# Another order for the first block's units, and numerators between gate and value, in a fused attention and feed-forward kernel

## The chip, the cores and the metric

The kernel runs on one core of a Trainium2 chip. The metric is the device time of one execution in microseconds. The kernel before takes 328.98 us, the median of three runs (328.57 to 329.07).

The core has five engines that run at the same time, each with its own queue in program order: TensorE (PE in the profile, its weight loads PEld), VectorE (DVE), ScalarE (ACT), GpSimd (POOL) and SyncE (SP), which here only issues transfers. They wait for each other by semaphores. TensorE writes to PSUM, a memory of eight banks of 512 fp32 values in each of 128 partitions.

## The reference

```
q, k, v: [8, 8, 576, 64]        # batch, heads, sequence, head size
phi(x) = [relu(x) cos(w), relu(x) sin(w)]    # w = pi/2 * pos/576, 128 features
kv  = phi(k)^T v                # per batch and head, 128 x 64
z   = sum over positions of phi(k)
num = phi(q) kv;  den = phi(q) z + 1e-6
x   = num / den, heads side by side          # [4608, 512]
g = x w_gate;  val = x w_val                 # 512 -> 1536
out = (gelu(g) * val) w_out                  # 1536 -> 512, float32
```

## The kernel before

The 4608 tokens of x are cut into nine blocks: block 0 has the 576 tokens of batch 0, blocks 1 to 7 have 512 tokens each, and block 8 the last 448 (`starts`, `ends`, L44). x is kept transposed, `xT`, with 512 features in four groups of 128 partitions.

**Feed-forward.** A unit is one of the 12 tiles of 128 hidden features (`jt`) for a stretch of tokens of a block. `gate` (L213) runs four matmuls into one PSUM bank and lets ScalarE take the gelu of it into a `gel` buffer, of which three rotate. `value` (L224) runs four matmuls into another bank, and VectorE multiplies that bank by the `gel` buffer into `hT` (L233). `gv_unit` is a gate and then a value; a list `mid` of functions can be called between the two, and nothing passes one in the kernel before. `o_tile` multiplies 128 tokens of `hT` by `w_out` (L258), ScalarE copies the bank, and SP stores it.

**Attention.** For each batch, `scale` computes phi for k and q (L134 on VectorE, L136 on ScalarE), and `cast_v` the bf16 values with a column of ones. `kv_half` computes kv and z for four heads in a bank (L153). A numerator step is `numer` (L192): `numer_mm` (L167, its matmuls L169) runs four matmuls of 65 columns into each of two neighbouring banks; then `norm` on VectorE takes the denominators (den, L181), their reciprocals (rec, L183) and the quotient (xb, L184). xb must be transposed to become a part of xT. In block 0 and for batch 1 this is done by PE (`x_by_pe`, L342, with a copy out of the bank in L345); for later batches SP issues a DMA transpose (`turn_x`, L204). The features of q are transposed in the same two ways (`q_by_pe` with `q_evac`, L323 and L331; `turn_q`, L144).

**Order.** All of it is written out by hand: the program order of each engine is that of the code. Block 0 begins while the weights are still being loaded by POOL in pieces (`load_w`: tiles 0 and 1, then 2 and 3, 4 to 7, 8 to 11). So its first units are small pieces of 128 tokens, each run as soon as its part of xT is there, from L408. There, `X(t, ...)` is the transpose of xb of token tile t, `Y(t, bank)` is the numerator step of tile t in that bank and the next, A stands for tokens 0 to 255 and `Bw` for 256 to 575. From tile 4 on a loop (L467) runs the remaining units in the two pieces A and Bw. Then comes the attention of batch 1, interleaved with the output tiles of block 0.

In blocks 1 to 6, `run_block(n)` runs the 12 units, gate banks 0 and 1, value banks 2 and 3 in turn. After each unit it calls what `after[n][jt]` holds: scales, transposes and loads of a later batch, `attn_step(b, 0)` (the two `kv_half`, banks 6 and 7), then in five further units `attn_step(b, i)` (a numerator step in banks 6 and 7 and its `turn_x`), and output tiles of the block before. In block 1 everything is one unit earlier, and the load of the next q comes in unit 5.

Buffers exist once for q, k and v in fp32 (`qf`, `kf`, `vf`), so a load is issued when the last reader is done. `dummies` are matmuls on a zeroed buffer `junk` that fill PE's waits at the start.

Of the kernel before, what the change touches and what calls it, by code (L numbers as in the profile page):

```python
# [9 lines left out]
FP32 = mybir.dt.float32  # L10
BF16 = mybir.dt.bfloat16
# [5 lines left out]
def kernel(  # L17
# [18 lines left out]
    JT = J // 128  # L36
# [9 lines left out]
    NB = len(starts)  # L46

    ctx.enter_context(tc.manual_schedule())
    sb = ctx.enter_context(tc.tile_pool(name="sb", bufs=1))
    rot = ctx.enter_context(tc.tile_pool(name="rot", bufs=2))  # L50
# [16 lines left out]
    kv = [sb.tile([128, H, D + 2], BF16, name=f"kv{i}") for i in range(2)]  # L67

    hT = [sb.tile([128, JT, 64 + 576], BF16, name=f"hT{i}") for i in range(2)]
    ident = sb.tile([128, 128], BF16, name="ident")  # L70
    junk = sb.tile([128, 512], BF16, name="junk")
    tiny = sb.tile([1, 8], FP32, name="tiny")


# [54 lines left out]
    def scale(f, j, which, eng, h0=0, h1=H):  # L129
        dst, src = f  # L130
        col = (cos_c if which == 0 else sin_c)[:, j:j + 1]
        s, d = src[:, h0:h1, j, :], dst[:, j, h0:h1, which * D:(which + 1) * D]
        if eng == "v":
            nc.vector.tensor_scalar(d, s, col, 0.0, op0=ALU.mult, op1=ALU.max)  # L134
        else:
            nc.scalar.activation(d, s, AF.Relu, scale=col)  # L136
# [55 lines left out]
    def numer(b, t, bank, rows=128):  # L192

        numer_mm(b, t, bank, 0, rows)
        numer_mm(b, t, bank, 1, rows)
        xb = new_xb()
        norm(xb, bank, 0, 2, rows)
        return xb
# [12 lines left out]
    gels = {}  # L211

    def gate(n, jt, c0, w, gb):  # L213

        p0 = starts[n] + c0
        for ct in range(CT):
            nc.tensor.matmul(  # L217
                ps[:, gb, 0:w], lhsT=wg_sb[:, ct, jt * 128:(jt + 1) * 128],
                rhs=xT[:, ct, p0:p0 + w], start=(ct == 0), stop=(ct == CT - 1),
            )  # L220
        gels[n, jt, c0] = gel = rot.tile([128, 512], FP32, name="gel", bufs=3)
        nc.scalar.activation(gel[:, 0:w], ps[:, gb, 0:w], AF.Gelu)  # L222

    def value(n, jt, c0, w, vb):  # L224

        p0 = starts[n] + c0
        for ct in range(CT):
            nc.tensor.matmul(  # L228
                ps[:, vb, 0:w], lhsT=wv_sb[:, ct, jt * 128:(jt + 1) * 128],
                rhs=xT[:, ct, p0:p0 + w], start=(ct == 0), stop=(ct == CT - 1),  # L230
            )
        gel = gels.pop((n, jt, c0))
        nc.vector.tensor_mul(hT[n % 2][:, jt, 64 + c0:64 + c0 + w], gel[:, 0:w], ps[:, vb, 0:w])  # L233

    def gv_unit(n, jt, c0, w, gb, vb, mid=()):
        gate(n, jt, c0, w, gb)
        for f in mid:
            f()
        value(n, jt, c0, w, vb)

    def carry(n):

        w = ends[n] - starts[n]
        nc.gpsimd.tensor_copy(hT[(n + 1) % 2][:, :, 0:64], hT[n % 2][:, :, w:w + 64])  # L244
# [74 lines left out]
    def q_by_pe(b, j, bank, eng, h0=0, h1=H):  # L319

        qb = ps[:, bank, :].bitcast(BF16).rearrange("p (h t) -> p h t", h=H)
        for h in range(h0, h1):
            nc.tensor.transpose(out=qb[:, h, :], in_=qp[:, j, h, :], identity=ident)  # L323
        if eng is not None:
            q_evac(b, j, bank, eng, h0, h1)

    def q_evac(b, j, bank, eng, h0=0, h1=H):
        qb = ps[:, bank, :].bitcast(BF16).rearrange("p (h t) -> p h t", h=H)
        cp = nc.vector.tensor_copy if eng == "v" else nc.scalar.copy
        if j < NJ:  # L330
            cp(qT[b % 2][:, j, h0:h1], qb[:, h0:h1])  # L331
        else:
            cp(qT[b % 2][:, j, h0:h1, 0:64], qb[:, h0:h1, 0:128:2])

    def x_by_pe(b, t, xb, bank, eng, c0=0, c1=CT, every=1):
        p0 = b * S + t * 128
        cp = nc.vector.tensor_copy if eng == "v" else nc.scalar.copy
        xb2 = xb.rearrange("p g h d -> p (g h d)")
        rows = 128 if t < NJ or every == 2 else 64
        view = ps[:, bank, 0:256].bitcast(BF16).rearrange("p (c t) -> p c t", c=CT)  # L340
        for ct in range(c0, c1):
            nc.tensor.transpose(  # L342
                out=view[:, ct, 0:rows], in_=xb2[0:rows, ct * 128:(ct + 1) * 128], identity=ident[0:rows, 0:rows],
            )
        cp(xT[:, c0:c1, p0:p0 + rows // every], view[:, c0:c1, 0:rows:every])  # L345

    def sq(j, which, eng, *h):
        scale(Q, j, which, eng, *h)
# [48 lines left out]
    A, Bw = (0, 256), (256, 320)  # L397
    xs = {1: x1}

    def X(t, bank, eng):  # L400
        return lambda: x_by_pe(0, t, xs[t], bank, eng)

    def Y(t, bank):
        def f():
            xs[t] = numer(0, t, bank, 128 if t < NJ else 64)
        return f

    gate(0, 0, 0, 128, 5)  # L408
    gate(0, 1, 0, 128, 4)
    X(1, 2, "v")()  # L410
    q_evac(0, 2, 3, "v")
    sq(3, 0, "v"), sq(3, 1, "s")
    value(0, 0, 0, 128, 6)
    value(0, 1, 0, 128, 7)
    gate(0, 0, 128, 128, 5)
    gate(0, 1, 128, 128, 4)
    sq(4, 1, "s"), sq(4, 0, "v")
    value(0, 0, 128, 128, 6)
    value(0, 1, 128, 128, 7)
    Y(2, 2)()  # L420
    q_by_pe(0, 3, 0, "s")
    q_by_pe(0, 4, 1, "v")
    gv_unit(0, 2, *A, 4, 6)
    X(2, 0, "s")()
    Y(3, 2)()
    gv_unit(0, 3, *A, 5, 7)
    gv_unit(0, 0, 256, 128, 4, 6)
    X(3, 1, "v")()
    Y(4, 2)()
    gv_unit(0, 1, 256, 128, 5, 7)  # L430
    gv_unit(0, 0, 384, 128, 4, 6)
    gv_unit(0, 1, 384, 128, 5, 7)
    X(4, 0, "v")()
    gate(0, 4, *A, 3)
    gv_unit(0, 2, *Bw, 4, 6)
    gv_unit(0, 3, *Bw, 5, 7)
    value(0, 4, *A, 1)
    gv_unit(0, 0, 512, 64, 0, 2)
    gv_unit(0, 1, 512, 64, 4, 6)


    load_q(1, nc.gpsimd)
# [7 lines left out]
    def L(f, *a):  # L450
        return lambda: f(*a)
# [14 lines left out]
    }  # L466
    for jt in range(4, 12):  # L467
        for i, (c0, w) in enumerate((A, Bw)):
            if (jt, i) != (4, 0):
                gv_unit(0, jt, c0, w, i, 3 - i)  # L470
            for f in between.get((jt, i), ()):
                f()
# [49 lines left out]


    after = {n: {jt: [] for jt in range(JT)} for n in range(NB)}
    for n in range(1, 7):
        b = n + 1
        a = after[n]

        def put(u, *fs):
            a[u].extend(fs)  # L530

        s = 0 if n > 1 else -1
        if n > 1:
            put(0, L(sq, 0, 0, "v"), L(sq, 1, 0, "v"), L(sq, 1, 1, "v"), L(sq, 0, 1, "s"))
            put(1, L(sq, 2, 0, "v"), L(sq, 2, 1, "s"), L(turn_q, b, 0, 3))
            put(1, L(sq, 3, 0, "v"), L(sq, 4, 0, "v"), L(sq, 4, 1, "v"), L(sq, 3, 1, "s"), L(turn_q, b, 3, 5))
        else:
            put(0, L(sq, 1, 1, "s"), L(sq, 2, 1, "v"), L(turn_q, b, 0, 3))
            put(0, L(sq, 3, 1, "v"), L(sq, 4, 1, "s"), L(turn_q, b, 3, 5))
        put(2 + s, L(sk, 0, 0, "v"), L(sk, 1, 0, "v"), L(sk, 0, 1, "s"), L(sk, 1, 1, "s"))  # L540
        put(3 + s, L(sk, 2, 0, "v"), L(sk, 3, 0, "v"), L(sk, 4, 0, "v"))
        put(3 + s, L(sk, 2, 1, "s"), L(sk, 3, 1, "s"), L(sk, 4, 1, "s"), L(cast_v, b, 0, 4))
        put(4 + s, L(cast_v, b, 4, 8, "s"))
        put(5 + s, L(attn_step, b, 0))
        if b + 1 < B:

            for f, u in zip((load_q, load_k, load_v), (3, 4, 5) if n > 1 else (5, 10, 11)):
                put(u, L(f, b + 1))
        for i in range(5):
            put(6 + s + i, L(attn_step, b, i + 1))  # L550

    for n in range(2, NB):
        for i, m in enumerate(o_tiles_of(n - 1)):
# [2 lines left out]
    def run_block(n):  # L556
        w = ends[n] - starts[n]
        for jt in range(JT):
            gv_unit(n, jt, 0, w, jt % 2, 2 + jt % 2)
            for f in after[n][jt]:  # L560
                f()
        if n + 1 < NB:
            carry(n)

    for n in range(1, NB):
        run_block(n)
# [34 lines left out]
```

## Time and profile before

| | us |
|---|---|
| median of three runs | 328.98 |
| the profiled execution's own time | 328.85 |
| its span | 326.7 |
| PE busy | 316.8 |
| DVE busy | 172.1 |
| ACT busy | 150.4 |
| POOL busy | 21.5 |

The span is the time from the first to the last recorded instruction; what lies around it is in the execution's own time only. Matmuls overlap: each is shown for 0.38 us at 512 columns, while four follow each other in 0.86 us, so a PE that is shown as busy may still be late, and start times are what to read. A row of the timeline has the start in us from the span's start, the length in us, the engine, the line, the operation, what it writes and reads, the count that was merged, and in brackets the idle time before it with the work that ended it. A row of the waits has the engine and line that waited, what for, the sum in us, how often, and the longest.

### The profile page before, as it was taken

The page shows a single profiled execution, that of the slowest core. Times are in us where ns is not written, and L with a number is a line of the kernel's source. Part 1 is how long each engine was busy: PE and PEld are TensorE (multiplying, and loading weights), DVE is VectorE, ACT ScalarE, POOL GpSimd, SP SyncE. Part 2 cuts the span into 40 slices and gives each one's busy share as a digit, 9 for nine tenths or more (in the row PEclk, how much of TensorE's full clock was granted, in tenths as well). Part 3 has the DMA queues.
Part 4 walks back from the last instruction along what each step waited for, and adds up shares of the span by engine and source line. Part 5 has one row for each costly group of instructions (what it writes and reads, how often), then busy time and mean ns, then how long its engine had stood idle before and what let it go on. Part 6 is the DMA issues. An engine that isn't in the chain of part 4 may idle for free.

```text
span 326.7 us, 5828 instructions
## 1 busy us (share of the span) xinstructions
PE 316.8 (97%) x2188; PEld 167.4 (51%) x2222; DVE 172.1 (53%) x383; ACT 150.4 (46%) x269; POOL 21.5 (7%) x41
## 2 busy tenths in 40 slices
PE   7999999999999999999999999999999999999994
PEld 2587866554445544544454445444554444444543
DVE  5795676868753667365835484548455222322210
ACT  6564664772474256424652375237622332223321
POOL 2650010000100010001000010001000100100000
PEclk9999999999999999999999999999999999999999
DMA  7999999996799938992699459984623211000024
GB/s 228 284 205 274 222 302 299 315 220 122 216 269 293 283 69 162 305 272 67 131 300 294 81 104 232 341 132 84 144 52 78 44 36 34 32 32 32 34 65 96
DMA packets 87739, 55.42 MB, mean 170 GB/s; under 512 B 52512, under 2 KB 82976, under 8 KB 87712
## 3 DMA queue, kind: packets, MB, share of 16 engines
q1 hardware_dynamic: 81200, 48.71, 59.7%
q0 software_dynamic: 6080, 5.90, 10.1%
q10 hardware_dynamic: 432, 0.46, 0.4%
q8 instruction: 17, 0.28, 0.3%
q14 instruction: 10, 0.08, 0.1%
HBM read 37.75 MB, written 9.44 MB: 144 GB/s over the span
## 4 chain that ended last, share of the span: by engine, by line
PE 91%; DVE 3%; DMA 2%; issue 1%; SPq 1%; POOL 0%; ACT 0%; DVEq 0%; POOLq 0%
PE ps L217 28%; PE ps L258 28%; PE ps L228 27%; PE ps L169 3%; PE ps L153 3%; DMA vf<-in_v_dram 2%; SPq L79 1%; DVE hT L233 1%; PE ps L276 1%; PE ps L342 1%; PE ps L323 1%; DVE xb L184 1%; DVE qp L134 0%; DVE rec L183 0%; DVE vx L140 0%
## 5 line engine op out<-in xcount | busy, mean ns | idle before, releaser
L233 DVE TENSOR_TENSOR hT<-gel,ps 128x512 bf16<-128x512 f32 (+5 forms) x126 | 76.4, 610 | 128.6 <-PE ps L228 121.8
L228 PE MATMUL ps<-xT,wv_sb 128*128 128x512 bf16 (+5 forms) x492 | 111.8, 348 | 1.1 <-DVE hT L233 0.8
L217 PE MATMUL ps<-xT,wg_sb 128*128 128x512 bf16 (+5 forms) x490 | 111.8, 348 | 1.0
L222 ACT ACTIVATE gel<-ps 128x512 f32<-128x512 f32 (+5 forms) x126 | 67.5, 536 | 77.6 <-PE ps L217 75.3
L258 PE MATMUL ps<-wo_sb,hT 128*128 128x512 bf16 x413 | 95.5, 379 | 0.6
L228 PEld LDWEIGHTS <-wv_sb 128*128 128x128 bf16 x504 | 47.9, 98 | 47.1 <-issue 1.0
L217 PEld LDWEIGHTS <-wg_sb 128*128 128x128 bf16 x504 | 45.7, 98 | 40.6 <-DVE xT L345 0.4
L258 PEld LDWEIGHTS <-hT 128*128 128x128 bf16 x420 | 40.1, 98 | 45.4
L287 ACT COPY o_sb<-ps 128x512 f32<-128x512 f32 x35 | 20.5, 585 | 75.4 <-PE ps L258 74.4
L184 DVE TENSOR_TENSOR xb<-ps,rec 128x512 bf16<-128x512 f32 (+2 forms) x41 | 27.8, 678 | 1.7 <-DVE rec L183 0.2
L136 ACT ACTIVATE kp<-kf,sin_c 128x512 bf16<-128x512 f32 (+1 forms) x41 | 25.4, 681 | 0.2 <-DMA kf<-in_k_dram 0.2
L134 DVE TENSOR_SCALAR qp<-qf,cos_c 128x512 bf16<-128x512 f32 x40 | 20.2, 546 | 0.0
L169 PEld LDWEIGHTS <-qT 128*128 128x128 bf16 (+1 forms) x320 | 15.0, 98 | 9.1 <-issue 2.3
L136 ACT ACTIVATE qp<-qf,sin_c 128x512 bf16<-128x512 f32 x28 | 19.3, 713 | 0.2 <-DMA qf<-in_q_dram 0.2
L134 DVE TENSOR_SCALAR kp<-kf,cos_c 128x512 bf16<-128x512 f32 (+1 forms) x45 | 18.7, 463 | 0.8 <-DMA kf<-in_k_dram 0.7
L169 PE MATMUL ps<-kv,qT 128*128 128x65 bf16 (+1 forms) x320 | 16.5, 193 | 0.5 <-DVE xb L184 0.3
L208 POOL COPY xT<-xr 128x256 bf16<-128x256 bf16 x6 | 2.4, 400 | 200.4 <-DMA xr<-xb 200.4
L153 PEld LDWEIGHTS <-kp 128*128 128x128 bf16 x320 | 10.9, 97 | 2.9 <-issue 1.0
L126 PE MATMUL ps<-junk 128*128 128x512 bf16 x33 | 10.5, 470 | 1.8 <-DVE par_i L103 1.7
L153 PE MATMUL ps<-vx,kp 128*128 128x65 bf16 x320 | 11.1, 193 | 0.4 <-DVE vx L140 0.4
L140 ACT CAST vx<-vf 128x1280 bf16<-128x1280 f32 (+1 forms) x9 | 9.7, 1076 | 1.6 <-DMA vf<-in_v_dram 1.6
L244 POOL COPY hT<-hT 128x768 bf16<-128x768 bf16 x8 | 7.6, 946 | 37.9 <-DVE hT L233 37.9
(55 smaller groups left out, 88.3 us busy)
## 6 DMA issues: line engine op xcount, KB each, us to landing
out_dram<-o_sb SPq DMA_DIRECT2D x38, 128.0 KB, 2.4
kf<-in_k_dram SPq DMA_DIRECT2D x7, 640.0 KB, 7.9
out_dram<-o_sb SPq DMA_DIRECT2D x16, 256.0 KB, 3.2
qf<-in_q_dram SPq DMA_DIRECT2D x6, 640.0 KB, 6.1
vf<-in_v_dram SPq DMA_DIRECT2D x6, 640.0 KB, 9.5
kf<-in_k_dram SPq DMA_DIRECT2D x7, 512.0 KB, 6.4
qf<-in_q_dram SPq DMA_DIRECT2D x6, 512.0 KB, 5.0
vf<-in_v_dram SPq DMA_DIRECT2D x6, 512.0 KB, 8.5
```

The source lines that it names most:

```text
L126: nc.tensor.matmul(ps[:, bank, :], lhsT=junk[:, 0:128], rhs=junk, start=True, stop=True)
L134: nc.vector.tensor_scalar(d, s, col, 0.0, op0=ALU.mult, op1=ALU.max)
L136: nc.scalar.activation(d, s, AF.Relu, scale=col)
L153: nc.tensor.matmul(ps[:, bank, (h % 4) * (D + 1):(h % 4 + 1) * (D + 1)], lhsT=kp[:, j, h, :], rhs=vx[b % 2][:, j, h, 0:D + 1], start=(j == ...
L169: nc.tensor.matmul(ps[0:rows, bank + g, (h % 4) * (D + 1):(h % 4 + 1) * (D + 1)], lhsT=qT[b % 2][:, t, h, 0:rows], rhs=kv[b % 2][:, h, 0:D ...
L184: nc.vector.tensor_tensor(xb[0:rows, g0:g1], nd[:, :, :, 0:D], rec[0:rows, 0:n, :, None].to_broadcast([rows, n, 4, D]), op=ALU.mult,)
L217: nc.tensor.matmul(ps[:, gb, 0:w], lhsT=wg_sb[:, ct, jt * 128:(jt + 1) * 128], rhs=xT[:, ct, p0:p0 + w], start=(ct == 0), stop=(ct == CT - 1),
L222: nc.scalar.activation(gel[:, 0:w], ps[:, gb, 0:w], AF.Gelu)
L228: nc.tensor.matmul(ps[:, vb, 0:w], lhsT=wv_sb[:, ct, jt * 128:(jt + 1) * 128], rhs=xT[:, ct, p0:p0 + w], start=(ct == 0), stop=(ct == CT - 1),
L233: nc.vector.tensor_mul(hT[n % 2][:, jt, 64 + c0:64 + c0 + w], gel[:, 0:w], ps[:, vb, 0:w])
L258: nc.tensor.matmul(ps[:, bank, :], lhsT=hT[n % 2][:, jt, c0:c0 + 128], rhs=wo_sb[:, jt, :], start=(jt == 0), stop=(jt == JT - 1),)
L287: nc.scalar.copy(o_sb, ps[:, bank, :])
```

## The change

Four things change.

1. In block 0 the hand-written order of the first units is another one. The numerators of tile 2 are put ahead of the second gates, those of tile 3 between gate and value of unit 3. The numerators use banks 0 and 1 in place of 2 and 3, transposes and values other banks too, and gates keep to 4 and 5 nearly throughout. Some copies out of PSUM go from VectorE to ScalarE and the other way. The A piece of tile 5 is run there too, so that the loop skips it.
2. In blocks 1 to 6 the five numerator steps with their `turn_x` are called between gate and value of their unit, and no longer after it.
3. `gel` has four buffers in place of three.
4. `junk` is no buffer of its own but a part of `hT[1]`.

On SP one step moves: in block 1 the first `turn_x` comes ahead of the two transfers of `load_q(3)`.

```diff
+    junk = hT[1][:, 0, 0:512]
     ident = sb.tile([128, 128], BF16, name="ident")
-    junk = sb.tile([128, 512], BF16, name="junk")
...
-        gels[n, jt, c0] = gel = rot.tile([128, 512], FP32, name="gel", bufs=3)
+        gels[n, jt, c0] = gel = rot.tile([128, 512], FP32, name="gel", bufs=4)
...
     gate(0, 0, 0, 128, 5)
     gate(0, 1, 0, 128, 4)
-    X(1, 2, "v")()
+    X(1, 2, "s")()
     q_evac(0, 2, 3, "v")
     sq(3, 0, "v"), sq(3, 1, "s")
     value(0, 0, 0, 128, 6)
     value(0, 1, 0, 128, 7)
+    Y(2, 0)()
     gate(0, 0, 128, 128, 5)
     gate(0, 1, 128, 128, 4)
+    value(0, 0, 128, 128, 2)
+    value(0, 1, 128, 128, 3)
+    q_by_pe(0, 3, 6, "s")
+    gate(0, 2, *A, 5)
+    X(2, 0, "v")()
     sq(4, 1, "s"), sq(4, 0, "v")
-    value(0, 0, 128, 128, 6)
-    value(0, 1, 128, 128, 7)
-    Y(2, 2)()
-    q_by_pe(0, 3, 0, "s")
-    q_by_pe(0, 4, 1, "v")
-    gv_unit(0, 2, *A, 4, 6)
-    X(2, 0, "s")()
-    Y(3, 2)()
-    gv_unit(0, 3, *A, 5, 7)
-    gv_unit(0, 0, 256, 128, 4, 6)
-    X(3, 1, "v")()
-    Y(4, 2)()
-    gv_unit(0, 1, 256, 128, 5, 7)
-    gv_unit(0, 0, 384, 128, 4, 6)
-    gv_unit(0, 1, 384, 128, 5, 7)
+    value(0, 2, *A, 7)
+    gate(0, 3, *A, 4)
+    Y(3, 0)()
+    value(0, 3, *A, 2)
+    q_by_pe(0, 4, 3, "s")
+    gv_unit(0, 0, 256, 128, 5, 6)
+    X(3, 0, "s")()
+    Y(4, 0)()
+    gv_unit(0, 1, 256, 128, 4, 7)
+    gv_unit(0, 0, 384, 128, 5, 2)
+    gv_unit(0, 1, 384, 128, 4, 3)
+    gate(0, 4, *A, 5)
     X(4, 0, "v")()
-    gate(0, 4, *A, 3)
-    gv_unit(0, 2, *Bw, 4, 6)
-    gv_unit(0, 3, *Bw, 5, 7)
-    value(0, 4, *A, 1)
-    gv_unit(0, 0, 512, 64, 0, 2)
-    gv_unit(0, 1, 512, 64, 4, 6)
+    gate(0, 5, *A, 4)
+    gv_unit(0, 2, *Bw, 1, 6)
+    gv_unit(0, 3, *Bw, 0, 7)
+    value(0, 4, *A, 3)
+    value(0, 5, *A, 2)
+    gv_unit(0, 0, 512, 64, 4, 6)
+    gv_unit(0, 1, 512, 64, 5, 7)
...
-            if (jt, i) != (4, 0):
+            if (jt, i) not in ((4, 0), (5, 0)):
                 gv_unit(0, jt, c0, w, i, 3 - i)
...
+    mid = {n: {jt: [] for jt in range(JT)} for n in range(NB)}
...
         for i in range(5):
-            put(6 + s + i, L(attn_step, b, i + 1))
+            mid[n][6 + s + i].append(L(attn_step, b, i + 1))
...
-            gv_unit(n, jt, 0, w, jt % 2, 2 + jt % 2)
+            gv_unit(n, jt, 0, w, jt % 2, 2 + jt % 2, mid[n][jt])
```

## The prediction

> **What bounds the kernel now.** I read the page's busy times first, then the chain that ended last, then busy time by stage, the waits of TensorE (PE) and the timeline around them.
>
> ```profile
> span 326.7 us, 5828 instructions
> PE 316.8 (97%) x2188; PEld 167.4 (51%) x2222; DVE 172.1 (53%) x383; ACT 150.4 (46%) x269; POOL 21.5 (7%) x41
> ...
> PE 91%; DVE 3%; DMA 2%; issue 1%; SPq 1%; POOL 0%; ACT 0%; DVEq 0%; POOLq 0%
> ```
>
> PE is the bound almost everywhere. Only time in which PE does not issue can be won. By stage (columns: stretch, its length, busy us and count of each engine, clock, DMA share, GB/s):
>
> ```profile
> 0.00:16.60 16.60, 14.07 (x117) 7.20 (x119) 11.17 (x40) 10.39 (x20) 7.67 (x21) 1.00 1.00 255
> 16.60:33.25 16.65, 15.70 (x204) 12.95 (x202) 11.58 (x34) 8.52 (x22) 4.05 (x6) 1.00 1.23 239
> ...
> 60.20:83.90 23.70, 23.27 (x175) 11.86 (x177) 17.98 (x40) 14.00 (x24) 0.00 (x0) 1.00 0.81 189
> 83.90:117.50 33.60, 33.34 (x220) 16.57 (x224) 18.60 (x40) 16.18 (x27) 1.17 (x2) 1.00 1.00 263
> 117.50:273.00 155.50, 154.46 (x976) 75.70 (x993) 82.80 (x169) 70.64 (x118) 6.62 (x10) 1.00 0.65 151
> ```
>
> A busy PE can still be late, because matmuls overlap. So I went by start times: a 512-column matmul should follow the last by 0.216 us (four in 0.86), 320 columns by 0.136, 256 by 0.109, 128 by 0.056, 65 by 0.032. A longer step is a stall. Single steps of twice the length, with a record missing, are not counted. The first stage (to 16.60) is not touched by the order of the change. After 273 nothing is.
>
> **Blocks 1 to 6.** The waits view between 60 and 270 us has, for PE and its weight loads, only the numerators (L169):
>
> ```profile
> PEld L169 <- issue: 1.9, 7, 0.6
> ```
>
> The costliest one, in block 1:
>
> ```profile
> 72.39 0.69 DVE L233 TENSOR_TENSOR hT<-gel,ps 128x512 bf16<-128x512 f32 x1 [2.23 <-PE ps L169]
> 72.87 1.03 PE L228 MATMUL ps<-xT,wv_sb 128*128 128x512 bf16 x4
> 73.00 0.16 DVE L181 TENSOR_SCALAR den<-ps 128x8 f32<-128x8 f32 x1
> ...
> 73.43 0.69 DVE L184 TENSOR_TENSOR xb<-ps,rec 128x512 bf16<-128x512 f32 x1
> ...
> 74.17 0.42 PE L169 MATMUL ps<-kv,qT 128*128 128x65 bf16 x8 [0.28 <-DVE xb L184]
> ```
>
> The four value matmuls from 72.87 end their issue at 72.87 + 0.864 = 73.73. The next numerator starts at 74.17, after xb (end 74.12) has emptied banks 6 and 7: 0.44 lost. The same sum at the other six places gives 0.07 (77.9), 0.07 (109.0), 0.26 (142.8), 0.07 (176.4), 0.07 (210.0), 0.07 (243.7): **1.05 us**. The 0.44 and 0.26 are larger because DVE itself started late there (product at 72.39 where 72.0 was possible; 0.23 idle between rec and xb at 142.05).
>
> **Block 0, 16.6 to 33.25.**
>
> ```profile
> 19.28 0.61 PE L228 MATMUL ps<-xT,wv_sb 128*128 128x128 bf16 x8 [0.56 <-DVE hT L233]
> ...
> 23.61 0.40 PE L342 MATMUL ps<-ident,xb 128*128 128x128 bf16 x4
> 23.93 0.44 PE L169 MATMUL ps<-kv,qT 128*64 128x65 bf16 x8
> ...
> 25.84 0.38 PE L228 MATMUL ps<-xT,wv_sb 128*128 128x128 bf16 x4 [0.24 <-DVE hT L233]
> ```
>
> Late steps: 0.13 (X(1) waits for x1, 17.18), 0.24 (gate waits for xT, 18.10), 0.73 (value of unit 0 waits until bank 6 is multiplied out, 19.28), 0.50 in six steps around the 64-row numerator and transpose of t=4 (23.6 to 26.9), 0.40 (bank 6 again, 25.84), 0.24 (bank 1, 30.20): **2.24 us**. Blocks 0 and 1 to 6 together offer 3.3 us, 1% of the time.
>
> **The Trainium skill.** "TensorE: Matmul & The Clock Gate", section Back-to-back issue gap, puts a warm gap at N/2.4 + 2.5 ns, 216 for 512 columns. The trace agrees (0.86 per four). "PSUM — Partial Sum Buffer", section Engine vs sequencer instructions: ScalarE and VectorE queues are strict FIFO, and matmuls run in program order. So a late product delays everything behind it, as at 19.28. The same page, section PSUM bank collisions, asks to guard a bank as a whole; the kernel's waits are of that kind (value on bank 6 waits for the product that reads it). "DMA: Bandwidth & Descriptors", section Queues, rings and completion order: each DMA engine consumes a queue's descriptors in ring order. In block 2 the first xT transpose, issued at 104.38 behind the loads of v, landed after 9.1 us, right after them, where an unqueued one takes 2.4: it agrees.
>
> **The change, part by part.**
>
> *junk in hT[1], four gel buffers.* No instruction more, the same memset and 34 dummies. Cost 0: hT[1] is first written in block 0's carry at 46.7, long after the dummies. The fourth gel buffer lets gates 0,4 and 0,5 stay open.
>
> *Numerators between gate and value, blocks 1 to 6.* The same 240 matmuls. Call the gate's start G, in a unit without an output tile. The numerator runs G+0.86 to 1.12. DVE: den at 1.31, rec 1.50, xb 1.74 to 2.43 (spacings of the rows at 73.00); then the product, whose value ends issue at 1.98, from 2.35 to 3.04. The next numerator comes at 1.98+0.86 = G+2.84, the banks are free at 2.49: slack 0.35, where before it was missing 0.07. That also covers the 0.23 late start and all but about 0.02 of the 0.37 one. The product is 0.1 later than before against its value, but its bank is needed two units on. First numerator of a block: it now comes 0.86 earlier, right after one gate. In block 2 kv's second copy ends at 101.21, the gate's issue at 101.49, so 0.2 remains. qT for t=0 landed at 69.25 against a need at 70.9 (block 1), later blocks have 3 us. Gain **1.05**.
>
> One SP step moves: in block 1 load_q(3), two DMAs (1.25 + 0.65 us of issue), now stands behind the first xT transpose, which waits for xb. It goes from 69.03 to about 73.7. It lands about 79 to 81 instead of 76.5, needed at 85.4: hidden. Behind it queue the transposes 1 to 4. Number 3 gates block 2, whose first gate moves from 83.89 to 83.38. xb3 is ready at 78.4 (80.1 before). With 1.2 us of issue each and the queue emptied of q by 79 to 81, it lands about 81.3 to 83.0 (82.97 before). Cost 0, cover 0.4 to 2 us.
>
> *Block 0.* I laid the new order out with the trace's own steps: DVE 128-column product 0.20, 256 0.36 to 0.41, scale 0.40, xT copy 0.34, den to xb 1.0; ACT gelu 0.17 to 0.31, scale 0.62, xT copy 0.59 (row at 22.17), qT copy 0.91; from the last matmul 0.26 to ACT, 0.41 to a product; 0.06 back to PE. What is late then:
> - X(1) still waits for x1: 0.13. Its copy on ACT ends at 18.20, so the second gate starts at 18.26 after the numerator of t=2 ended at 18.12: 0.14.
> - value into banks 2 and 3 does not wait: the 0.73 is gone. gate(0,2) comes at 19.60; its weights landed at 19.2. value(0,2) comes at 20.27; those weights (issue 11.84, 8.3 to landing) at 20.1: free by 0.15.
> - X(3) waits for xb3, ready at 22.84: 0.10.
> - **Y(4,0) follows X(3,0) at once and uses its bank.** X(3) ends issue at 23.08; ACT starts its copy at 23.28 and ends at 23.87; the numerator starts at 23.93. **0.85 lost, a new wait.** The t=4 evacuation stands ahead on ACT at 22.49. Its row is only known on DVE (0.68). On ACT it lies between 0.59 (same elements) and 1.01 (the 1024-element copy); "ScalarE: Activation LUTs", Rules for kernel authors, prices 0.3 us + 0.83 ns per element, 0.73 here, an estimate. I take 0.59. At 1.01 the wait grows by 0.3; bounded below by 0.85, since ACT is free at 23.28.
> - Leaving the 64-row numerator 0.10, X(4) in and out 0.19, as before.
> - Bank 1 and 6 waits at 25.84 and 30.20 are gone. With (5,0) taken out, (4,1) and (5,1) follow each other on banks 1 and 2: gate waits for the gelu 0.16, value for the product 0.12: 0.28.
>
> Sum after: 0.13+0.14+0.10+0.85+0.10+0.19+0.28 = 1.79. Gain 2.24 - 1.79 = **0.45**. The load of q for block 1 is issued some 2 us later (sq(4) on ACT moves to 21.0), but it lay behind weights until 30.3 anyway, and is used at 36.1. k and v follow wo, which landed at 37.1 and 41.6 by DMA rate; with PE 0.45 earlier, the scales at 45.4 still find k (landed 44.7), the casts v (last half at 47.9, wanted at 49.5).
>
> Total 0.45 + 1.05 = 1.50 us. Span 326.7 to 325.2; the profiled execution's own time 328.85 (2.15 around the span) to 327.35; it lies 0.13 below the median 328.98. **Forecast 327.5.**
>
> **Rivals.** (1) The bank-0 chain in block 0 costs more than the order saves: 1.01 us for the evacuation and 0.5 more of weights arriving late turn +0.45 into about -0.3. For it: slack at 20.1 is only 0.15. Against: each term is a row. Total gain 0.75, 328.2. (2) DVE's late starts move rather than vanish, and a new wait of 0.07 stays: blocks give 0 to 0.5. Against: slack 0.35. 328.0 to 328.5. (3) The reverse: ACT frees bank 0 sooner than laid out or other waits hide it: gain 2.3, 326.7. (4) Slower: transpose 3 of block 1 lands late behind q. Each us past 83.4 is one us of stall, the gain is used up at 84.9, and from 85.5 it is slower by over 0.2%. For it: the 9.1 us transpose behind loads in block 2. Against: there 2.3 MB stood ahead, here 1.2 MB. At 86, 329.6 to 330. That the order does not change is excluded: PE's queue has the numerators between the gate's and the value's matmuls, with the same count.
>
> **Numbers.** Forecast 0.50 (its own range 327.2 to 327.9), (1) 0.15, (2) 0.13, (3) 0.08, (4) 0.14. 0.2% is 0.66 us, about what a measurement can tell from no change: faster means below 328.3, slower above 329.6. Faster: 0.48+0.10+0.05+0.08 = 0.71; slower 0.11 of (4); same 0.18. The range 326.7 to 329.2 leaves out most of (4) and the tip of (3).
>
> **What would show it.** No L169 wait in blocks 1 to 6, and xb ahead of the unit's hT on DVE. In block 0 no L228 wait at 19.3, one wait of L169 on ACT's xT copy of about 0.85 near 23.9, and 33.25 reached at 32.8. Wrong if block 2's first gate waits for xT, or if value(0,2) waits for DMA.

## The result, and the profile after

The changed kernel took 327.35 us (median of 4 runs, 327.04 to 328.16), the kernel before, run beside it, 329.02 us (4 runs, 328.57 to 329.18). The medians are 1.67 us apart. The ratio, which is nearer to that of the means (327.48 and 328.95), is 0.9955, 95% interval 0.9934 to 0.9976: 1.48 us, and 0.79 to 2.17 by the interval. The forecast was 327.5.

The profiled execution of the changed kernel is the longest of its four, 328.16 us with a span of 326.0; 33 of its matmul records are missing. So I profiled the same kernel once more (called "again" here, 327.73 us, the longest of its five executions; span 325.6, all records there). In the changed kernel all lines of the code stand one lower: numerators are L170, gates L218, values L229, products L234, xT copies L346.

The head of the page of the changed kernel, first profile, and its chain that ended last:

```profile
span 326.0 us, 5837 instructions
PE 315.3 (97%) x2189; PEld 166.8 (51%) x2222; DVE 169.1 (52%) x381; ACT 151.4 (46%) x271; POOL 20.8 (6%) x41
...
PE 91%; DMA 4%; POOL 1%; issue 1%; ACT 0%; SPq 0%; DVE 0%; POOLq 0%; ACTq 0%
```

The bound has not changed. On the chain, DVE has gone from 3% to 0 and DMA from 2% to 4%. By line, the DMA part is the weights of the value part (2.6%) and the first load of q (1.8%): in this execution the chain runs back through unit 2's wait for its weights in block 0, which is shown below.

Busy time by stage (same columns as in the prediction), first of the changed kernel's first profile, then of "again":

```profile
117.50:273.00 155.50, 154.55 (x978) 75.81 (x995) 80.61 (x168) 71.01 (x119) 6.07 (x10) 1.00 0.66 151
```

```profile
60.20:83.90 23.70, 23.23 (x177) 11.70 (x176) 18.26 (x40) 13.68 (x24) 0.17 (x1) 1.00 1.00 202
117.50:273.00 155.50, 155.50 (x996) 75.93 (x995) 80.17 (x168) 71.24 (x119) 5.85 (x10) 1.00 0.65 151
```

The first line would say that nothing was won after 117.5 (154.46 busy before, 154.55 after); but it counts 978 matmuls where 996 ran. With all records, PE is busy for every one of the 155.50 us. Between 60.2 and 83.9 "again" is idle for 0.47 us. That is a wait, as the waits view of "again" between 60 and 270 us shows (waiter, what ended the wait, us in total, times, longest). These two lines, the first for the weight loads and the second for the matmuls, are all it has there for TensorE:

```profile
PEld L218 <- issue: 0.9, 1, 0.9
...
PE ps L218 <- DMA xT<-xb: 0.5, 1, 0.5
```

No numerator waits any more between 60 and 270 us. In their place stands one gate, which waits for a transposing DMA of xT. The timeline of "again" shows which one:

```profile
82.02 1.03 PE L229 MATMUL ps<-xT,wv_sb 128*128 128x512 bf16 x4
...
83.51 0.81 PE L218 MATMUL ps<-xT,wg_sb 128*128 128x512 bf16 x3 [0.47 <-DMA xT<-xb]
```

It is the first gate of block 2. It could start at 82.02 + 0.864 = 82.88 and starts at 83.51: 0.63 lost, 0.32 in the first profile (at 83.95). The cause stands in the timeline of SP's queue of "again":

```profile
72.08 1.19 SPq L205 DMA_TRANSPOSE xT<-xb  x1
73.32 1.35 SPq L80 DMA_DIRECT2D qf<-in_q_dram  x2
74.78 4.35 SPq L205 DMA_TRANSPOSE xT<-xb  x3
```

Before, the two loads of q were issued at 69.03 and 70.33, and landed at 74.3 and 76.5. Now they go out at 73.32 and 74.03 and land at 77.5 and 80.2, and the three transposes behind them land at 82.3, 82.8 and 83.3. The gate wants the last of them.

The unit that had lost 0.44 us, in block 1, timeline of the first profile:

```profile
71.40 1.02 PE L229 MATMUL ps<-xT,wv_sb 128*128 128x512 bf16 x4
...
72.11 0.69 DVE L185 TENSOR_TENSOR xb<-ps,rec 128x512 bf16<-128x512 f32 x1
...
72.72 0.68 DVE L234 TENSOR_TENSOR hT<-gel,ps 128x512 bf16<-128x512 f32 x1
...
73.12 0.42 PE L170 MATMUL ps<-kv,qT 128*128 128x65 bf16 x8
```

The division comes before the product, ends at 72.80, and the next numerator at 73.12 follows its gate without a wait: slack 0.32, where the prediction had 0.35.

In block 0 the three lines around the wait that the prediction expected near 23.9 (first profile, in which the stage starts 0.41 later than before):

```profile
20.43 0.39 PE L343 MATMUL ps<-ident,xb 128*128 128x128 bf16 x4
21.05 0.61 PE L229 MATMUL ps<-xT,wv_sb 128*128 128x256 bf16 x4 [0.23 <-DMA wv_sb<-in_moe_w_val_dram]
...
23.58 0.40 PE L343 MATMUL ps<-ident,xb 128*128 128x128 bf16 x4
...
24.65 0.42 PE L170 MATMUL ps<-kv,qT 128*64 128x65 bf16 x8 [0.67 <-ACT xT L346]
```

The last of the four transposes starts at 23.76, so the numerator of t=4 could start 0.056 later, at 23.81, and starts at 24.65: 0.84 lost, predicted 0.85. The value of unit 2 at 21.05 waits 0.40 us for its weights; in "again" it starts at 20.32 and does not wait.

To compare executions I use the starts of the same matmuls in each trace (us), so that a late start of one stage is not put down to the next:

| stretch | before | after, first | after, again |
|---|---|---|---|
| start to first gate of block 0 | 16.60 | 17.01 | 16.67 |
| block 0: first gate to first output tile | 29.30 | 29.14 | 28.73 |
| to block 1's first gate | 14.29 | 14.28 | 14.29 |
| block 1: to block 2's first output tile | 27.15 | 26.96 | 27.27 |
| blocks 2 to 7: to the last value matmul | 224.27 | 223.75 | 223.76 |
| to the last matmul | 10.47 | 10.47 | 10.47 |
| last matmul to the end | 4.62 | 4.39 | 4.40 |

Before to "again": block 0 gives 0.57, block 1 loses 0.12, the blocks from 2 on give 0.51, the end gives 0.22. The first row is not touched by the order of the change and lay between 16.13 and 17.01 in the twelve traces of this study. That spread of 0.88 is near the 1.12 between the four times of the changed kernel, so the comparisons below rest on medians for the total and on the other rows for the place.

### The profile page after: what moved, and what is told of

Same layout as the page of the kernel before. It is cut to its first block, busy times and chain, and to the rows that moved or that the text cites. A ratio compares the mean times of both kernels' runs of the same rounds, so it can differ in the third digit from the quotient of the medians.

```text
span 326.0 us, 5837 instructions
## 1 busy us (share of the span) xinstructions
PE 315.3 (97%) x2189; PEld 166.8 (51%) x2222; DVE 169.1 (52%) x381; ACT 151.4 (46%) x271; POOL 20.8 (6%) x41
## 4 chain that ended last, share of the span: by engine, by line
PE 91%; DMA 4%; POOL 1%; issue 1%; ACT 0%; SPq 0%; DVE 0%; POOLq 0%; ACTq 0%
PE ps L229 28%; PE ps L218 28%; PE ps L259 28%; PE ps L170 3%; DMA wv_sb<-in_moe_w_val_dram 3%; PE ps L154 3%; DMA qf<-in_q_dram 2%; PE ps L277 1%; PE ps L343 1%; POOL wg_sb L305 0%; PE ps L324 0%; SPq L80 0%; POOL wv_sb L306 0%; ACT xT L346 0%; POOL vf L98 0%
## 5 line engine op out<-in xcount | busy, mean ns | idle before, releaser
L234 DVE TENSOR_TENSOR hT<-gel,ps 128x512 bf16<-128x512 f32 (+5 forms) x126 | 75.9, 607 | 88.7 <-PE ps L229 86.9
L229 PE MATMUL ps<-xT,wv_sb 128*128 128x512 bf16 (+5 forms) x498 | 112.1, 348 | 0.6 <-DMA wv_sb<-in_moe_w_val_dram 0.2
L218 PE MATMUL ps<-xT,wg_sb 128*128 128x512 bf16 (+5 forms) x490 | 111.7, 348 | 0.9 <-issue 0.2
L259 PE MATMUL ps<-wo_sb,hT 128*128 128x512 bf16 x408 | 94.1, 379 | 0.6
L218 PEld LDWEIGHTS <-wg_sb 128*128 128x128 bf16 x504 | 47.0, 98 | 45.3 <-issue 0.8
L229 PEld LDWEIGHTS <-wv_sb 128*128 128x128 bf16 x504 | 45.6, 98 | 39.6 <-DMA wv_sb<-in_moe_w_val_dram 0.4
L182 DVE TENSOR_SCALAR den<-ps 128x8 f32<-128x8 f32 (+2 forms) x41 | 6.7, 165 | 43.9 <-PE ps L170 43.9
L170 PEld LDWEIGHTS <-qT 128*128 128x128 bf16 (+1 forms) x320 | 15.1, 98 | 8.7 <-issue 1.0
L135 DVE TENSOR_SCALAR qp<-qf,cos_c 128x512 bf16<-128x512 f32 x40 | 18.1, 495 | 0.0
L170 PE MATMUL ps<-kv,qT 128*128 128x65 bf16 (+1 forms) x320 | 16.6, 194 | 0.8 <-ACT xT L346 0.7
L127 PE MATMUL ps<-hT 128*128 128x512 bf16 x33 | 9.2, 427 | 1.8 <-DVE par_i L104 1.7
```

The costliest lines, as they stand in the source:

```text
L170: nc.tensor.matmul(ps[0:rows, bank + g, (h % 4) * (D + 1):(h % 4 + 1) * (D + 1)], lhsT=qT[b % 2][:, t, h, 0:rows], rhs=kv[b % 2][:, h, 0:D ...
L218: nc.tensor.matmul(ps[:, gb, 0:w], lhsT=wg_sb[:, ct, jt * 128:(jt + 1) * 128], rhs=xT[:, ct, p0:p0 + w], start=(ct == 0), stop=(ct == CT - 1),
L229: nc.tensor.matmul(ps[:, vb, 0:w], lhsT=wv_sb[:, ct, jt * 128:(jt + 1) * 128], rhs=xT[:, ct, p0:p0 + w], start=(ct == 0), stop=(ct == CT - 1),
L259: nc.tensor.matmul(ps[:, bank, :], lhsT=hT[n % 2][:, jt, c0:c0 + 128], rhs=wo_sb[:, jt, :], start=(jt == 0), stop=(jt == JT - 1),)
```

## The experiments

The theory after the result: the numerators' waits are gone as predicted, block 0 pays a new 0.84 for bank 0, and the moved load of q costs a new wait in block 1. Rivals: the gain is from the two buffer edits; or VectorE's late starts were only shifted to other places; or the weights for unit 2 are the limit of block 0. The kernel before had a median of 328.84, 328.86 and 328.80 us in the three comparisons (the first: the next four runs; the second: bank 7 for X(3), unit 2's weights, the three edits, and the buffers; the third: alternating banks and the four memsets).

### The changed kernel again

No edit.

> The changed kernel itself, once more, as the yardstick for the runs beside it. Theory P (the prediction's sum: 0.45 us from block 0, 1.05 us from blocks 1 to 6, less 0.3 us that the first profile shows as a new wait ahead of block 2): 1.2 to 1.7 us below the kernel before. Theory S (the profiled execution, with its 0.4 us wait of value(0,2) for weights and its late start, is the typical one): 0.7 to 0.9 us below.

327.39 us, ratio 0.9954 [0.9942, 0.9966]. It repeats the result, and its profile is the one to compare the others with.

### The numerators alone

The kernel before, with only this:

```diff
+    mid = {n: {jt: [] for jt in range(JT)} for n in range(NB)}
...
-            put(6 + s + i, L(attn_step, b, i + 1))
+            mid[n][6 + s + i].append(L(attn_step, b, i + 1))
...
-            gv_unit(n, jt, 0, w, jt % 2, 2 + jt % 2)
+            gv_unit(n, jt, 0, w, jt % 2, 2 + jt % 2, mid[n][jt])
```

> Only the numerators of blocks 1 to 6 moved between gate and value, block 0 as before. Theory P: 1.05 us of numerator waits gone, 0.3 us of a new wait for xT at block 2's first gate: 0.7 to 0.8 us faster than before. Theory S says the same of this part. Rival R (DVE's late starts only move): 0 to 0.4 us faster. The trace should show no wait of L170's counterpart on DVE between 60 and 270 us.

327.94 us, ratio 0.9975 [0.9964, 0.9986]: 0.90 faster. The stretches: block 0 29.30 as before, block 1 27.23 (0.08 worse), blocks 2 to 7 223.76 (0.51 better), end 4.40 (0.22 better). The first gate of block 2 waits 0.48 here too, and one numerator 0.10 at 72.8. So this half brings its wait for xT with it, without the other half.

### Block 0 alone

The changed kernel, with the numerators put back behind the value part:

```diff
-            mid[n][6 + s + i].append(L(attn_step, b, i + 1))
+            put(6 + s + i, L(attn_step, b, i + 1))
...
-            gv_unit(n, jt, 0, w, jt % 2, 2 + jt % 2, mid[n][jt])
+            gv_unit(n, jt, 0, w, jt % 2, 2 + jt % 2)
```

> Only block 0's new order, the banks, the four gel buffers and junk in hT[1]; numerators after the value as before. Theory P: 0.45 us faster (a range of 0.2 to 0.9, by whether value(0,2) waits for its weights). Theory S: 0.0 to 0.2 us faster. The block-0 stretch should show the 0.85 us wait of the 64-row numerator on ScalarE's copy of xT.

327.85 us, ratio 0.9971 [0.9961, 0.9982]: 0.99 faster, more than the 0.2 to 0.9 that had been expected. Block 0 took 28.99 (0.31 better, with 0.25 lost to unit 2's weights). But it also moved stages in which it changes no instruction: block 1 took 26.78 (0.37 better), blocks 2 to 7 took 224.44 (0.17 worse), the end 4.39 (0.23 better). The 0.44 in block 1 had shrunk to 0.07, and a new one of 0.35 appeared; its line in the timeline:

```profile
143.98 0.41 PE L170 MATMUL ps<-kv,qT 128*128 128x65 bf16 x8 [0.19 <-DVE xb L185]
```

The halves alone sum to 1.89, together they give 1.45. The end's 0.22 is in both and counts once, and so is block 1's late start of 0.37, which either half removes. The 0.17 that block 0 alone loses in blocks 2 to 7 is not lost together (223.76). 1.89 - 0.22 - 0.37 + 0.17 = 1.47, which 1.45 meets; the intervals reach some 0.35 us to each side.

### load_q(3) ahead of the first transpose

The changed kernel, with this:

```diff
-                put(u, L(f, b + 1))
+                if n == 1 and u == 5:
+                    mid[n][u].append(L(f, b + 1))
+                else:
+                    put(u, L(f, b + 1))
```

> The changed kernel with the two transfers of load_q(3) ahead of block 1's first xT transpose again, as in the kernel before. Theory Q (q's transfers behind that transpose made the later transposes, and so block 2's first gate, late): that gate waits for nothing, and the kernel is 0.3 us faster than the changed one beside it. Rival: the transposes are late because PE is early or the rings are full anyway; then the wait stays and the time is that of the changed kernel within 0.1 us.

327.16 us, ratio 0.9948 [0.9936, 0.9960]. By the times alone it is not told apart from the changed kernel (327.39, intervals overlap). The trace tells. SP's queue, and PE at the first gate of block 2:

```profile
69.45 1.83 SPq L80 DMA_DIRECT2D qf<-in_q_dram  x2
72.11 7.40 SPq L205 DMA_TRANSPOSE xT<-xb  x4
```

```profile
82.05 1.03 PE L229 MATMUL ps<-xT,wv_sb 128*128 128x512 bf16 x4
...
82.92 1.03 PE L218 MATMUL ps<-xT,wg_sb 128*128 128x512 bf16 x4
```

q lands at 74.6 and 77.0, the transposes at 77.5, 79.5, 80.0 and 80.8, 2.1 us ahead of the gate, which starts 0.87 after the value: no wait. TensorE waits nowhere between 60 and 270 us, and block 1 took 26.65 against 27.27. The place of two load instructions on SP's queue is worth up to 0.62 us. In two of the executions below which keep the moved load, this wait is absent (in one of them the transpose landed at 82.56, 0.4 before the gate), so it costs between 0 and 0.63 from one execution to the next.

### X(3) into bank 7

The changed kernel, with this:

```diff
-    X(3, 0, "s")()
+    X(3, 7, "s")()
     Y(4, 0)()
-    gv_unit(0, 1, 256, 128, 4, 7)
-    gv_unit(0, 0, 384, 128, 5, 2)
+    gv_unit(0, 1, 256, 128, 4, 2)
+    gv_unit(0, 0, 384, 128, 5, 7)
```

> The changed kernel with the transpose of x tile 3 in bank 7 in place of bank 0, and values (0,1,256) in bank 2 and (0,0,384) in bank 7. Theory B (the 64-row numerator waits 0.84 us only because ScalarE's copy of tile 3 reads its bank 0): that wait shrinks to about 0.1 us, the rest being ScalarE's evacuation of q's tile 4, and the kernel is 0.7 us faster than the changed one, about 1.0 us if nothing later takes it back. Rival L (the first value units then wait for weights or, after block 0, for the loads of k and v): 0 to 0.3 us faster, with the wait seen elsewhere.

326.60 us, ratio 0.9929 [0.9915, 0.9943]: 0.8 better than the changed kernel. Its timeline:

```profile
22.56 0.59 ACT L334 COPY qT<-ps 128x512 bf16<-128x512 bf16 x1 [0.65 <-PE ps L324]
22.86 0.40 PE L343 MATMUL ps<-ident,xb 128*128 128x128 bf16 x4
23.20 0.44 PE L170 MATMUL ps<-kv,qT 128*64 128x65 bf16 x8
23.30 0.59 ACT L346 COPY xT<-ps 128x512 bf16<-128x512 bf16 x1
```

With another bank the numerator starts before ScalarE's copy of X(3) has begun: it is due at 22.86 + 0.22 = 23.08 and starts at 23.20, about 0.1 late where it was 0.84. Only banks were changed, so the 0.84 is bank 0. Block 0 took 28.19 against 28.73; 0.15 of the difference went to a wait of unit 2's value for its weights. That matches "Perfetto Trace Analysis", Matmuls, of the Trainium skill: independent matmul groups should rotate through different banks, so that the evacuation of one overlaps the matmuls of the next.

### Unit 2's value without its own weights

The changed kernel, but value(0, 2) multiplies by tile 0's weights, so that part of the output is another:

```diff
-    def value(n, jt, c0, w, vb):
+    def value(n, jt, c0, w, vb, wj=None):
...
-    value(0, 2, *A, 7)
+    value(0, 2, *A, 7, 0)
```

> The changed kernel in which value(0,2) of tokens 0 to 255 multiplies by the value weights of tile 0 in place of tile 2, so that it needs no weights that are still on their way; that part of the output is then another. Theory W (the 0.40 us wait in the first profile is a matter of when the weights land in that execution): within 0.2 us of the changed kernel's median. Rival: the wait is there in most executions, and the kernel is 0.3 to 0.4 us faster.

327.18 us, ratio 0.9946 [0.9933, 0.9959]. Value (0,2) does not wait, and block 0 took 28.74, the same as "again", where the weights came in time. So these weights cost 0 to 0.40 from execution to execution (they landed at 21.01, 19.89, 20.17 and 20.29 in the traces of the changed kernel, "again", block 0 alone and bank 7), and no more than some 0.2 of the median. That is at the edge of the 0.2 us that had been expected, under the rival's 0.3 to 0.4, and the intervals prove neither.

### Three edits together

The edits of "load_q(3) ahead" and "X(3) into bank 7", and this:

```diff
-                gv_unit(0, jt, c0, w, i, 3 - i)
+                g = 0 if jt == 5 else i
+                gv_unit(0, jt, c0, w, g, 3 - g)
```

> Three edits on the changed kernel together: load_q(3) ahead of block 1's first transpose, x tile 3 in bank 7, and unit (5,1) on banks 0 and 3 in place of 1 and 2 (so that it does not follow unit (4,1) on the same banks, 0.27 us of waits). Theory: 0.3 to 0.6 + 0.7 + 0.27 us, so 1.3 to 1.6 us faster than the changed kernel, near 326.0 us. Rival L: the loads of k and v for batch 1, which follow the weights at the rate of the transfers, bound the stretch to 51 us: 0.5 to 0.9 us faster, and TensorE waits at the kv matmuls of batch 1.

326.49 us, ratio 0.9926 [0.9913, 0.9939], no better than bank 7 alone: 0.9 faster than the changed kernel where 1.3 to 1.6 had been expected. The load of q could give nothing over bank 7's profiled execution, in which block 2's gate did not wait. Rival L is not the reason: TensorE waits nowhere between 43 and 51 us. The new edit was a miss: (5,1) now has bank 0, free by then, but (6,0) after it wants bank 0 as well. PE's timeline:

```profile
31.23 0.71 PE L229 MATMUL ps<-xT,wv_sb 128*128 128x320 bf16 x4
31.92 0.60 PE L218 MATMUL ps<-xT,wg_sb 128*128 128x256 bf16 x4
32.59 0.60 PE L229 MATMUL ps<-xT,wv_sb 128*128 128x256 bf16 x4
```

Steps of 0.69 and 0.67 where 4 x 0.136 = 0.54 and 4 x 0.109 = 0.44 are due: 0.38 lost, where the changed kernel loses 0.27 one unit earlier. The wait had only been moved.

### Alternating banks to the end of block 0

As the run above, but:

```diff
-                g = 0 if jt == 5 else i
+                g = 1 - i if jt > 4 else i
```

> load_q(3) first, x tile 3 in bank 7, and from hidden tile 5 on all the rest of block 0 on the other pair of banks, so that no two units in a row have the same pair. (With unit (5,1) alone on the other pair, unit (6,0) followed it on the same banks and waited 0.38 us.) Theory: those waits are gone, 0.38 us faster than with that edit, 0.27 us faster than without it: near 326.2 us. Rival L (the loads of k and v for batch 1 bound the stretch): the time stays at 326.5 us and VectorE or TensorE waits between 43 and 51 us.

326.00 us, ratio 0.9917 [0.9905, 0.9929], 2.8 us faster than before and the fastest kernel here. The same place:

```profile
30.80 0.71 PE L229 MATMUL ps<-xT,wv_sb 128*128 128x320 bf16 x4
31.34 0.60 PE L218 MATMUL ps<-xT,wg_sb 128*128 128x256 bf16 x4
31.78 0.60 PE L229 MATMUL ps<-xT,wv_sb 128*128 128x256 bf16 x4
```

0.54 and 0.44, no wait, and none between 43 and 51 us, where rival L would have had one. Block 0 took 27.87 (29.30 before, 28.73 in "again"), and 1.4 us of the 2.8 are won there.

### The buffers alone

The kernel before, with only this:

```diff
-    junk = sb.tile([128, 512], BF16, name="junk")
+    junk = hT[1][:, 0, 0:512]
...
-        gels[n, jt, c0] = gel = rot.tile([128, 512], FP32, name="gel", bufs=3)
+        gels[n, jt, c0] = gel = rot.tile([128, 512], FP32, name="gel", bufs=4)
```

> The kernel before with only the four gel buffers and junk in hT[1]. Theory P: within 0.1 us of the kernel before. Rival: the place of the buffers or the fourth gel buffer itself gives part of the gain: 0.2 us or more faster.

328.92 us, ratio 1.0001 [0.9992, 1.0009]. Every stretch from block 0 on is within 0.02 of before. The two edits only make room; alone they neither cost nor give anything.

### Four more VectorE instructions

The kernel before, with this ahead of the first Gelu:

```diff
+    pad = sb.tile([1, 8], FP32, name="pad")
+    for i in range(4):
+        nc.vector.memset(pad[0:1, i:i + 1], 0.0)
```

> The kernel before with four one-element memsets more on VectorE, put where it waits for the first k. Theory F (VectorE's late starts, 0.37 us at 72.0, 0.2 us at 142.0 and 0.23 us at the program's end, belong to places in its stream of instructions, not to the work there): they turn up at other instructions or vanish, so 0.2 to 0.8 us faster. Rival: they belong to the work; they stay, and the time is that of the kernel before within 0.1 us.

328.50 us, ratio 0.9990 [0.9981, 0.9998]: four added instructions made it 0.30 faster. The order of the work is that of before. The timeline at the two places that had lost 0.44 and 0.26 (four lines more in the code: L172 is the numerator, L231 the value, L187 the division):

```profile
73.10 1.03 PE L231 MATMUL ps<-xT,wv_sb 128*128 128x512 bf16 x4
...
74.03 0.41 PE L172 MATMUL ps<-kv,qT 128*128 128x65 bf16 x8
...
141.54 1.03 PE L231 MATMUL ps<-xT,wv_sb 128*128 128x512 bf16 x4
...
142.83 0.41 PE L172 MATMUL ps<-kv,qT 128*128 128x65 bf16 x8 [0.27 <-DVE xb L187]
```

Less 0.864 each, the numerators lose 0.07 (0.44 before) and 0.43 (0.26 before). The end of the program went from 4.62 to 4.41. Block 0 has a new wait:

```profile
20.30 0.48 DVE L236 TENSOR_TENSOR hT<-gel,ps 128x128 bf16<-128x128 f32 x2 [0.35 <-PE ps L172]
...
23.85 0.40 PE L345 MATMUL ps<-ident,xb 128*128 128x128 bf16 x4
```

The first of these products does not need the numerator (L172) that the view names. It starts 0.45 after the step before it, where before it was 0.05; VectorE stays behind up to xb of tile 3, and the transposes of X(3) start 0.16 late. Block 0 took 29.41 against 29.30. In sum 0.37 - 0.17 + 0.21 - 0.11 = 0.30, the 0.30 of the medians.

The traces also say where the late starts are. Count all instructions that a trace records for VectorE, those included that only wait for a semaphore and that the timeline leaves out. The late ones of the kernel before are number 192 (72.39), 320 (142.05), 448 (212.65) and 576 (326.37, at the program's end): 128 apart. With four instructions more they are number 64 (20.30) and 320 (141.05), at other work. In the twelve traces, seventeen instructions after the first microsecond start more than 0.1 us after VectorE was free and the last signal that they wait for had come, and every one of them has the number 64, 192, 320, 448 or 576. Not each such number is late: in "again" number 192 is a division right behind its reciprocal and starts on time. So these late starts go with the place in VectorE's stream and not with the work around them.

## Why the prediction was right, and where it was not

**The sum.** Forecast 327.5 and a gain of 1.50; measured 327.35 and 1.67, 1.45 when repeated. The total is right, in part by luck: load_q(3) and unit 2's weights cost up to 0.63 and 0.40 in an execution where the sum had 0, and the end gave 0.23 that the sum did not have. The prediction had named two signs of being wrong, block 2's first gate waiting for xT and value(0,2) waiting for DMA. Both are in the first profile.

**Numerators in blocks 1 to 6, "Gain 1.05": right in every place.** None of the seven waits is left in "again", and with load_q ahead TensorE waits nowhere in that stretch. Blocks 2 to 7 gave 0.51, against 0.07 + 0.26 + 0.07 + 0.07 + 0.07 = 0.54. The slack of 0.35 was 0.32. (The second of the seven numerators, put at 77.9, started at 78.20; its 0.07 is right.) Block 1 held the other 0.51, and it was won: with load_q ahead its stretch is 26.65, 0.50 below before. One point the prediction could not see: 0.37 of block 1's share and 0.2 of block 3's were late starts that shift with VectorE's stream. Without the numerators' new place they come back elsewhere (143.98 with block 0 alone). With it the slack covers them, wholly or nearly: with bank 7 for X(3), the products that are number 320 and 448 start 0.24 later than their like and no numerator waits; with the numerators alone, number 192 is the den at 71.59, 0.37 late, and the next numerator loses 0.10. So only the 7 x 0.07 is surely due to the order; the rest is insurance against late starts, and what that pays depends on where they fall.

**load_q(3) behind the first transpose, "Cost 0, cover 0.4 to 2 us": wrong.** It costs 0 to 0.63. This is rival 4's mechanism, at its small end. The step that failed is "it lands about 81.3 to 83.0": transpose 3 landed at 83.3 and 83.7. I had worked the transposes as four issues of 1.2 us behind a queue that q had left. In fact q's second load landed at 80.2 and 82.1, and all three transposes landed after it, 0.5 us apart, 2.1 us later in "again" and 0.65 in the first profile. The gate's time was off as well: 83.38 was worked out with the 0.51 of block 1 alone and left out what block 0 gives, so PE was there at 82.88. The Trainium skill's statement, cited in the prediction, that each DMA engine consumes a queue's descriptors in ring order, agrees as far as it goes. It doesn't give the 2.1 us, and why one execution has 2.1 and another 0.65 stays open. The profile had the warning, 9.1 us for a transpose behind loads in block 2; I set it aside for its larger load.

**Block 0, "Gain 0.45": right, low by 0.1.** With the weights in time it gave 0.57. The terms, predicted and measured (first profile or "again"): X(1) 0.13, 0.13; second gate 0.14, 0.14; X(3) 0.10, 0.06; bank 0 0.85, 0.84; the 64-row steps 0.29, 0.29; (4,1) and (5,1) 0.28, 0.27. Sum 1.79 and 1.73. The new wait on bank 0 came out to 0.01 because ScalarE's copy for t=4 took 0.59, the value I took (0.586 on average); the 0.73, an estimate from the skill's rule, was too high here. That rule is given for an instruction whose bias is a pointer operand, which the prediction left out. Bank 7 for X(3) shows that the wait was this and could be had back. Rival 1 rested on a longer evacuation and on late weights; the first fell, the second came in some executions and at 0.40 at most.

The matmul spacing that the prediction took from the Trainium skill also holds less widely there than it was put. "TensorE: Matmul & The Clock Gate", Back-to-back issue gap, gives N/2.4 + 2.5 ns for an isolated matmul, and about 131 ns at 512 columns for a stream of weight loads and matmuls; here the stream ran at 216, so the measurement decides for the formula.

**value(0,2) "free by 0.15": right on average, no margin.** It was free in "again", and missed by 0.40, 0.25, 0.15 and 0.09 in four other executions. Not a wrong number, but a slack smaller than the scatter of a landing (19.89 to 21.01); a cost of about 0.1 to 0.2 would have been the fair entry. Its 0.40 in the first profile goes with a late start of the whole execution: the first gate started 0.41 late, q had landed 0.77 later than before, and the weights' first issue, which waits for q, came at 10.04 instead of 9.27. The 0.25 with block 0 alone came without such a start (first issue at 9.34).

**Buffers, "Cost 0": right.** Alone, 1.0001.

**What no step had: the end, 0.23.** After the last matmul everything takes as long as before up to the last stores. Then the program's closing instructions run, and before VectorE's last of these (a drain) ran at 326.37, 0.47 us after it was released (325.90); after, at 325.53, 0.09 after (325.44). GpSimd's last steps wait for it. That is 0.23 us that no edit aimed at: both halves alone have it, and so do the four memsets; the buffers do not. The drain is number 576 of VectorE's instructions before and with the buffers alone, and has another number in every other run. Without it the gain would have been about 1.2 to 1.4.

## What to carry to other kernels

A numerator, whose banks must be emptied before the next one, was better placed between gate and value than after both: the slack that it gained (0.32) is worth more than the regular 0.07, since it also covers late starts that nobody planned. It is worth trying for any group of that kind. When an order is moved on one engine, list what else the moved step used to let go first: here two loads on SP's queue changed places with a transpose, and the transposes behind them set the next block's start. Two groups in a row on one bank wait for the evacuation between them (0.84 us for X(3) and the numerator here, 0.27 at the end of block 0), and a slack below the scatter of a transfer (1.1 us here) is not a slack.

## What was unexpected of the hardware

VectorE starts single instructions 0.2 to 0.4 us late with nothing to wait for, and in these twelve traces only at every 128th of its recorded instructions: number 64, 192, 320, 448 and 576. Four memsets far ahead took one wait of TensorE from 0.44 to 0.07, made another 0.43 out of 0.26, made a new one of 0.16 in block 0 and removed the late start at the program's end. Why the places lie 128 apart stays open (a fetch of instructions would fit, but no run tested it), and so does why some of these instructions start on time. The consequence is that a difference of 0.2 to 0.4 us between two kernels of this size need not come from the edit's purpose.
